# Attention and a two-layer network on one core: broadcast rows joined in one DRAM tile and fetched piece by piece behind the output's stores, and the float32 weight words stored after the split

## The chip, the core and the metric

The kernel runs on one core of a Trainium2 chip. A core has five engines that run their own instruction streams and meet only at semaphores: TensorE (PE in the profile, with its weight loads as PEld), VectorE (DVE), ScalarE (ACT), GpSimd (POOL) and SyncE (SP), which here does nothing but issue DMAs. All but three small loads at the start are issued by SP, in program order: a DMA that has to wait for a semaphore holds up every DMA behind it in SP's queue. The metric is the device time of one execution in microseconds (us), and less is better.

## The reference, cut to what matters

```python
# q, k, v: (4, 8, 768, 64); proj: (64, 6); moe_w_in: (512, 2048); moe_w_out: (2048, 512)
q_bits = (np.einsum('bhsd,dk->bhsk', q, proj) > 0); k_bits = ...   # 6 bits give a bucket
mask = q_bucket[:, :, :, None] == k_bucket[:, :, None, :]
scores = np.where(mask, scale * np.matmul(q, k.transpose(0, 1, 3, 2)), -1000000000.0)
attn = softmax(scores)                     # with 1e-09 added to the sum
attn_out = np.matmul(attn, v)
x = attn_out.transpose(0, 2, 1, 3).reshape(4 * 768, 512)
h = x @ w_in
g = np.where(h >= 1, h, np.where(h <= -1, 0.0, (h + 1) ** 2 / 4))
out = g @ w_out
```

The weights come as float64 and every product is formed from operands that are split into a rounded part and a remainder (hi and lo), so that one float32 product is three TensorE products.

## The kernel before, in words

**Attention.** 32 heads run one after another, each in 12 units (`NU`), about 14 us a head. At fixed units a list of tasks is worked off: moving the next pairs' operands (`move`, L154), putting the row maxima in place (`max_put`, L278: the row that the scores' second matmul needs, `t<-te`, and a copy to DRAM, `ed<-te`), and converting weights (`WeightSplit.steps`, L55). A conversion loads 64-bit words (`s0`), turns them into float32 in `wsq` with four DVE operations and one ACT operation (`s1` to `s4`), rounds (`s5`, ACT) and takes the remainder (`s6`, POOL). With `keep`, the float32 words are stored to DRAM too (`put`, L95, `wq<-wsq`), right behind `s4`. The twelve conversions with `keep` (L997) start at unit 0 of an odd head, and their `put` lies at unit 16 from there, which is unit 4 of the next, even head. Unit 3 of that head has two `move` of 384 KB each, and unit 5 has `max_put`.

**What attention leaves.** The unnormalised output goes to DRAM tiles `x_d[b]`, the maxima's rows to `e_d[b]`, and the inverse of the sums to `r_d[b]` (`sums_inv`), one row of 768 for each of 8 heads. The network's input is (x + e * sv) * r (`make`, L547, and `x_norm`, L698). For that the rows of e and r are read back spread over 64 partitions each: `load_er` (L533) and `x_er` (L689), one DMA of 96 KB for each of e and r, of two heads and of four pieces of 384 tokens, so 16 DMAs a call of `x_er`.

**Network, first stage** (L837, about 484 to 619 us). Chunks of 384 tokens; the first two chunks take 32 steps of 12 matmuls `h` (`gemm1`) and 9 matmuls `y` (L669) that lag three steps. ACT forms t and z from h (`act_in`, L625), DVE squares and adds (`act_out`, L632), ACT rounds (`g_hi`), DVE takes the remainder (`g_lo`). Before each step n the list `prep[n]` is worked off, after it `post[n]`.

**Network, second stage** (L876, 168 products k = 0 to 167, about 619 us to the end). The other six chunks, two a batch of 56 products; a group of seven products (s = 0 to 6, Strassen-like, with sums of operands) makes two blocks of h. Each product is six matmuls, then five or six `y` matmuls of earlier blocks. Two PSUM banks `hb` alternate, so a product needs what DVE or ACT reads two products before. The weights of each product (256 KB) come through a ring of nine buffers (`w_load`, L775).

**Order around the change.** `x_plan` (L719) puts the making of a batch's operands into `prep` and `post`: `x_raw` (four loads of x into `pc[0..3]`) and `x_er` at one place, `x_norm` for the four pieces, then sums, roundings and remainders at the places `made`. In the second stage x_raw and x_er stand at product 3 and 30 of the 56 (L828), `x_norm` from 4 products later, at every second product. When a chunk's `y` is complete, `flush` (L647) copies it from PSUM to SBUF on ACT and stores it (`out_dram<-ot`, 256 KB). For the first two chunks it has two buffers for three copies; later it has four buffers for six copies. The last two chunks' copies of a stage fall at products 4 and 5 (end of the first stage), and at products 2 to 5 of the next 56 (end of a batch).

SP's order inside a step is: the ring's load, the tasks of `prep`, then the stores of `flush`. Each DMA of `x_er` takes SP about 0.6 us to issue.

Of the kernel before, what the change touches and what calls it, by code (L numbers as in the profile page):

```python
# [22 lines left out]
P = 128  # L23
# [18 lines left out]
class WeightSplit:  # L42
# [10 lines left out]
    def steps(self, src, shape, hi, lo, cp, stage=None, low=None, keep=None):  # L53
# [43 lines left out]
        if stage is None:  # L97
            return [s0, s1, s2, s3, s4] + ([put] if keep is not None else []) + [s5, s6]
# [406 lines left out]
class XMaker:  # L505
# [3 lines left out]
    def __init__(self, nc, x_d, s_d, e_d, r_d):  # L509
        self.nc, self.x_d, self.s_d, self.e_d, self.r_d = nc, x_d, s_d, e_d, r_d  # L510
        self.sv, self.er, self.raw = {}, {}, {}

    def sums_load(self, sm, em, b):
# [3 lines left out]
        nc.sync.dma_start(out=self.em, in_=self.e_d[b].rearrange("h (a f) -> (h a) f", f=NF))  # L517
# [56 lines left out]
def ffn(ctx, tc, wpair, woh, wol, xm, xa, xb, areas, wst, wq, wc, out, prep, post):  # L574
# [13 lines left out]
    pc = [xp.tile([P, CH], F32, name=f"pc{i}") for i in range(6)]  # L588
# [20 lines left out]
    def spread(b, cc, k, t):  # L609

        n = 2 * k + t
        if b > 1:
            return sets[(b - 1) % 2][(14, 15, 16, 17, 18, 19, 25, 26)[n]].bitcast(F32)
        if cc == 1:
            return cut(ta, n).bitcast(F32)
        return cut(tflat, n).bitcast(F32) if n < 5 else cut(sflat, n - 5) if n < 7 else pc[5]
# [64 lines left out]
    def x_raw(b, cc):  # L681
# [435 lines left out]
```

## Time and profile before

| | |
|---|---|
| median of 3 runs | 1033.53 us (1033.2, 1033.53, 1037.53) |
| profiled execution: its time, its span | 1037.66 us, 1035.9 us |
| granted TensorE clock, mean | 0.99 |
| DMA: bytes, share of 16 engines | 166.19 MB, 56.6% |
| loads of the broadcast rows (`x_er`) | 96 DMAs of 96 KB |
| loads of the broadcast rows (`load_er`) | 32 DMAs of 96 KB |
| stores of the float32 words with `keep` | 12 of 16 `wq<-wsq` |
| busy share PE, DVE, ACT, POOL | 95%, 77%, 66%, 33% |

The profile comes from one execution; its span leaves out 1.8 us of that execution's time. A timeline row gives start, duration, engine, source line and output<-input; in square brackets stands the engine's idle time before it and what ended it. A row of waits gives the total, the number and the longest of the waits of one kind. A row of a stage gives the stage, its length, the busy time of each engine with the number of instructions, and then the granted TensorE clock, the DMA engines' share and GB/s.

### The profile page before, as it was taken

To read this page: it belongs to the slowest core of one execution; us is meant where nothing else is said; L and a number is where in the kernel's file an instruction comes from. 1 tells how busy PE (TensorE), PEld (TensorE's weight loads), DVE (VectorE), ACT (ScalarE), POOL (GpSimd) and SP (SyncE) were. 2 spreads that over 40 slices of the span, in tenths; PEclk is the share of its full clock that TensorE was granted. 3 is DMA by queue.
4 is the path that set the end of the run, shared out by engine and by line. 5 is a ranking of instruction groups with operands and counts; after the bars stand their busy time and mean duration, and the time that the engine had idled before them with its cause. 6 is when DMAs were issued, how large, how long until landed. Compare 5 with 4: busy or idle time off the path is not lost.

```text
span 1035.9 us, 15651 instructions
## 1 busy us (share of the span) xinstructions
PE 979.7 (95%) x5036; PEld 895.1 (86%) x5036; DVE 793.9 (77%) x1356; ACT 680.9 (66%) x1489; POOL 343.5 (33%) x412
## 2 busy tenths in 40 slices
PE   5899999999999999999998996999996999999997
PEld 4789989899999999989997885888986888988896
DVE  7678989899999998885878983877764767755553
ACT  5779878898989888887545563454553554554444
POOL 6667767777778777565000000000000000000000
PEclk9999999999999999999999998999998999999999
DMA  2645657676656666635376477667456455454331
GB/s 91 171 111 149 170 158 190 169 184 165 179 160 180 159 171 163 152 105 167 95 223 226 143 235 239 206 209 259 122 143 199 117 171 154 119 176 122 113 92 61
DMA packets 95449, 166.19 MB, mean 160 GB/s; under 512 B 15112, under 2 KB 52616, under 8 KB 95368
## 3 DMA queue, kind: packets, MB, share of 16 engines
q1 hardware_dynamic: 95152, 165.20, 56.6%
q8 instruction: 40, 0.66, 0.3%
q14 instruction: 41, 0.34, 0.1%
q10 hardware_dynamic: 216, 0.00, 0.0%
HBM read 106.13 MB, written 33.87 MB: 135 GB/s over the span
## 4 chain that ended last, share of the span: by engine, by line
PE 66%; DVE 10%; DMA 8%; ACT 7%; SPq 5%; issue 2%; POOL 1%; ACTq 0%; DVEq 0%
PE y L669 19%; PE h L892 14%; PE smax L258 5%; PE s L298 5%; PE o L332 5%; PE o L330 5%; PE o L331 5%; PE s L297 4%; DMA t<-te 4%; PE h L801 4%; SPq L695 3%; DVE nm L262 2%; DMA wraw<-in_w_in_dram 1%; DVE t L634 1%; ACT t L628 1%
## 5 line engine op out<-in xcount | busy, mean ns | idle before, releaser
L306 ACT ACTIVATE ph<-s 128x384 fp32r<-128x384 f32 x380 | 188.0, 495 | 55.3 <-PE s L298 47.8
L262 DVE TENSOR_REDUCE nm<-smax 128x1 f32<-128x768 f32 x186 | 176.4, 948 | 26.9 <-PE smax L258 25.4
L39 POOL TENSOR_TENSOR pl<-pf,ph 128x384 fp32r<-128x384 f32 x128 | 140.3, 1101 | 87.7 <-ACT pf L311 83.5
L634 DVE SCALAR_TENSOR_TENSOR t<-t 128x384 f32<-128x384 f32 x128 | 71.4, 557 | 107.2 <-ACT z L629 107.0
L39 DVE TENSOR_TENSOR pl<-s,ph 128x384 fp32r<-128x384 f32 x256 | 135.8, 545 | 14.7 <-ACT s L311 11.0
L669 PE MATMUL y<-t,ghi 128*128 128x512 f32 x384 | 126.5, 401 | 17.5 <-ACT ghi L639 17.4
L298 PE MATMUL s<-t 128*128 128x384 f32 x384 | 131.8, 343 | 6.2 <-DMA t<-te 6.0
L297 PE MATMUL s<-t 128*128 128x384 f32 x384 | 132.4, 345 | 0.8 <-DVE t L212 0.8
L332 PE MATMUL o<-pl,va 128*128 128x386 f32 x384 | 130.8, 341 | 0.2 <-DVE pl L39 0.2
L330 PE MATMUL o<-ph,va 128*128 128x386 f32 x384 | 130.6, 340 | 0.0
L331 PE MATMUL o<-ph,vb 128*128 128x386 f32 x384 | 130.1, 339 | 0.0
L311 ACT ACTIVATE s<-s 128x384 f32<-128x384 f32 x252 | 125.3, 497 | 0.0
L258 PE MATMUL smax<-t 128*128 128x384 f32 x372 | 101.5, 354 | 5.3 <-DVE nm L262 4.6
L669 PEld LDWEIGHTS y<-t,ghi 128*128 128x128 f32 x384 | 72.3, 191 | 29.3 <-ACT ghi L639 18.8
L639 ACT CAST ghi<-z 128x384 fp32r<-128x384 f32 x129 | 65.2, 506 | 34.0 <-DVE z L635 31.6
L643 DVE TENSOR_TENSOR glo<-z,ghi 128x384 fp32r<-128x384 f32 x128 | 70.4, 550 | 19.3 <-ACT ghi L639 19.3
L892 PE MATMUL h<-wbig,t 128*128 128x384 f32 x399 | 82.6, 340 | 0.5 <-DVE wsq L911 0.5
L258 PEld LDWEIGHTS smax<-t 128*128 128x128 f32 x372 | 64.5, 190 | 20.3 <-DVE nm L262 19.0
L629 ACT ACTIVATE z<-t,m 128x384 f32<-128x384 f32 x128 | 79.0, 617 | 4.2
L628 ACT ACTIVATE t<-wsq,mh 128x384 f32<-128x384 f32 x48 | 29.6, 617 | 79.1 <-DVE wsq L905 46.1
L298 PEld LDWEIGHTS s<-t 128*128 128x128 f32 x384 | 72.6, 189 | 10.3 <-DMA t<-te 10.3
L892 PEld LDWEIGHTS h<-wbig,t 128*128 128x128 f32 x399 | 72.3, 190 | 6.6 <-DVE wsq L911 1.4
(150 smaller groups left out, 2113.2 us busy)
## 6 DMA issues: line engine op xcount, KB each, us to landing
t<-wc SPq DMA_DIRECT2D x92, 256.0 KB
t<-t SPq DMA_DIRECT2D x60, 384.0 KB
wraw<-wc SPq DMA_DIRECT2D x76, 256.0 KB
raw<-in_qk_dram SPq DMA_DIRECT2D x15, 768.0 KB
wraw<-in_w_in_dram SPq DMA_DIRECT2D x16, 512.0 KB
wraw<-in_w_out_dram SPq DMA_DIRECT2D x16, 512.0 KB
xd<-xs SPq DMA_DIRECT2D x32, 192.5 KB
vraw<-in_v_dram SPq DMA_DIRECT2D x16, 384.0 KB
```

Source lines behind the costliest of these rows:

```text
L39: eng.tensor_tensor(out=out, in0=a, in1=b, op=ALU.subtract)
L258: nc.tensor.matmul(out=smax[hd][:, hf, 0:HS], lhsT=t2[:, 0, h, i * P:(i + 1) * P], rhs=t2[:, 1, h, hf * HS:(hf + 1) * HS], start=True, sto ...
L262: nc.vector.tensor_reduce(out=nmp(hd)[:, i:i + 1], in_=smax[hd][:, :, 0:HS], axis=AX.XY, op=ALU.max, negate=True)
L297: nc.tensor.matmul(out=ps[:, 0:HS], lhsT=t1[:, 1, h, ks], rhs=t1[:, 0, h, sl], start=True, stop=False)
L298: nc.tensor.matmul(out=ps[:, 0:HS], lhsT=t2[:, 1, h, ks], rhs=t2[:, 0, h, sl], start=False, stop=True)
L306: nc.scalar.activation(out=ph[:, 0:HS], in_=ps[:, 0:HS], func=AF.Exp, scale=SCALE)
L311: nc.scalar.activation(out=pf, in_=ps[:, 0:HS], func=AF.Exp, scale=SCALE)
L330: nc.tensor.matmul(out=o, lhsT=wa, rhs=ph, start=(jj == 0), stop=False)
L331: nc.tensor.matmul(out=o, lhsT=wb, rhs=ph, start=False, stop=False)
L332: nc.tensor.matmul(out=o, lhsT=wa, rhs=pl, start=False, stop=(jj == NJ - 1))
L669: nc.tensor.matmul(out=ys[c][m], lhsT=g_[:, m * P:(m + 1) * P], rhs=w, start=(first and k == 0), stop=(last and k == 2))
L892: nc.tensor.matmul(out=ps, lhsT=w[:, cs], rhs=x, start=(n == 0 and s not in (2, 3, 6)), stop=(n == 5), skip_group_check=True)
```

## The change

Four things are done.

1. `e_d[b]` and `r_d[b]` become the two halves of one DRAM tile `er_d[b]` of shape [8, 2, 768]. A piece's rows e and r of one head are then one DMA of 192 KB, so a call for a piece issues two DMAs in place of four. The SBUF targets are pairs of neighbouring blocks; the six tiles `pc` become one tile `pcs` with six slices, and `x_raw` issues two loads of 384 KB in place of four of 192 KB.
2. `x_er` works one piece k, and `x_plan` takes a place for each: 11, 12, 13, 14 in place of four at 11; 24, 24, 25, 25 in place of 24; in the second stage t, t+1, t+2, t+3.
3. In the second stage t goes from 3 and 30 to 7 and 31. `x_norm` stands at t+4 to t+7 in place of t+4, t+6, t+8, t+10, and `made` at t+9+2k in place of t+12+2k: places 16 to 28 (before 15 to 27) and 40 to 52 (before 42 to 54).
4. `put` with `keep` moves behind `s5` and `s6`: from unit 16 to unit 21, that is from unit 4 to unit 9 of the even head.

```diff
@@ WeightSplit.steps
-            return [s0, s1, s2, s3, s4] + ([put] if keep is not None else []) + [s5, s6]
+            return [s0, s1, s2, s3, s4, s5, s6] + ([put] if keep is not None else [])
@@ XMaker
-        nc.sync.dma_start(out=self.em, in_=self.e_d[b].rearrange("h (a f) -> (h a) f", f=NF))
+        nc.sync.dma_start(out=self.em, in_=self.er_d[b][:, 0].rearrange("h (a f) -> h a f", f=NF))
...
-        nc.sync.dma_start(out=self.r_d[b].rearrange("h (a f) -> (h a) f", f=NF), in_=sm)
+        nc.sync.dma_start(out=self.er_d[b][:, 1].rearrange("h (a f) -> h a f", f=NF), in_=sm)
...
-    def load_er(self, c, ct, eb, rb):
-        b, sl = c // 2, slice(c % 2 * CH, (c % 2 + 1) * CH)
+    def load_rows(self, b, ct, k, er):
+
         for h in range(2):
-            rs = slice(64 * h, 64 * h + 64)
-            r = 2 * ct + h
-            self.nc.sync.dma_start(out=eb[rs], in_=self.e_d[b][r:r + 1, sl].partition_broadcast(64))
-            self.nc.sync.dma_start(out=rb[rs], in_=self.r_d[b][r:r + 1, sl].partition_broadcast(64))
-        self.er[c, ct] = (eb, rb)
+            src = self.er_d[b][2 * ct + h:2 * ct + h + 1, :, k * CH:(k + 1) * CH]
+            self.nc.sync.dma_start(out=er[64 * h:64 * h + 64], in_=src.rearrange("o t n -> (o t) n").partition_broadcast(64))
+
+    def load_er(self, c, ct, er):
+        self.load_rows(c // 2, ct, c % 2, er)
+        self.er[c, ct] = (er[:, 0], er[:, 1])
@@ ffn
-    pc = [xp.tile([P, CH], F32, name=f"pc{i}") for i in range(6)]
+    pcs = xp.tile([P, 6, CH], F32, name="pcs")
+    pc = [pcs[:, n] for n in range(6)]
...
-        for k in range(4):
-            sl = slice(k // 2 * CH, (k // 2 + 1) * CH)
-            nc.sync.dma_start(out=pc[k], in_=xm.x_d[b][:, 2 * (k % 2) + cc, sl])
-
-    def x_er(b, cc):
-        for k in range(4):
-            ct, sl = 2 * (k % 2) + cc, slice(k // 2 * CH, (k // 2 + 1) * CH)
-            for t, d in enumerate((xm.e_d[b], xm.r_d[b])):
-                for h in range(2):
-                    r = 2 * ct + h
-                    nc.sync.dma_start(out=spread(b, cc, k, t)[64 * h:64 * h + 64],
-                                      in_=d[r:r + 1, sl].partition_broadcast(64))
+        for k in range(2):
+            nc.sync.dma_start(out=pcs[:, 2 * k:2 * k + 2], in_=xm.x_d[b][:, cc::2, k * CH:(k + 1) * CH])
+
+    def x_er(b, cc, k):
+        xm.load_rows(b, 2 * (k % 2) + cc, k // 2, spread(b, cc, k))
@@ x_plan and its calls
         at(raw, x_raw, b, cc)
-        at(er, x_er, b, cc)
         for k, n in enumerate(norm):
             at(n, x_norm, b, cc, k)
+            at(er[k], x_er, b, cc, k)
...
-    x_plan(1, 0, 11, 11, (13, 14, 15, 16), (17, 17, 18, 18, 19, 19, 20))
-    x_plan(1, 1, 22, 24, (26, 26, 27, 27), (28, 28, 29, 29, 30, 30, 31))
+    x_plan(1, 0, 11, (11, 12, 13, 14), (13, 14, 15, 16), (17, 17, 18, 18, 19, 19, 20))
+    x_plan(1, 1, 22, (24, 24, 25, 25), (26, 26, 27, 27), (28, 28, 29, 29, 30, 30, 31))
     for b in (2, 3):
         for cc in range(2):
-            t = N1 + 56 * (b - 2) + (3, 30)[cc]
-            x_plan(b, cc, t, t, [t + 4 + 2 * k for k in range(4)], [t + 12 + 2 * k for k in range(7)])
+            t = N1 + 56 * (b - 2) + (7, 31)[cc]
+            x_plan(b, cc, t, [t + k for k in range(4)], [t + 4 + k for k in range(4)],
+                   [t + 9 + 2 * k for k in range(7)])
@@ lsh_attn_ffn
-    e_d = [xdp.tile([H, S], F32, name=f"ed{b}") for b in range(B)]
+    er_d = [xdp.tile([H, 2, S], F32, name=f"ed{b}") for b in range(B)]
+    e_d = [t[:, 0] for t in er_d]
...
-        conv((2 * i + 3) * NU, wi_steps(i, nc.scalar), (0, 7, 9, 13, 15, 16, 17, 19))
+        conv((2 * i + 3) * NU, wi_steps(i, nc.scalar), (0, 7, 9, 13, 15, 17, 19, 21))
```

`spread` chooses the same SBUF memory for the rows as before in batches 2 and 3 and in the second call of batch 1. In the first call of batch 1 the third and fourth pieces move by one block, so that each pair is contiguous.

More of the change, by code (lines that the diff above doesn't have):

```diff
@@ L505, with __init__ @@
 class XMaker:
[L509 to L510 removed]
+    def __init__(self, nc, x_d, s_d, er_d):
+        self.nc, self.x_d, self.s_d, self.er_d = nc, x_d, s_d, er_d
         self.sv, self.er, self.raw = {}, {}, {}
@@ L952, in lsh_attn_ffn @@
     wc = [xdp.tile([P, NBLK, 2, DM // 2], F32, name=f"wc{i}") for i in range(NFT // 2)]
-    r_d = [xdp.tile([H, S], F32, name=f"rd{b}") for b in range(B)]
-    xm = XMaker(nc, x_d, s_d, e_d, r_d)
+    xm = XMaker(nc, x_d, s_d, er_d)
     def flat(t):
@@ L1028, in load_er @@
     def load_er(c, ct):
-        xm.load_er(c, ct, *(t[:, ct].bitcast(F32) for t in (xa, xb)[c]))
+        er = flat((T2[i0], T2[i1])[c]).rearrange("p (t c n) -> p t c n", t=2, c=NCT)
+        xm.load_er(c, ct, er[:, :, ct].bitcast(F32))
     at(g0 + 2, load_raw)
```

21 lines of the change are left out of this document (12 added, 9 removed).

## The prediction

> **What bounds the kernel now.** The page first: who is busy, and at what clock.
>
> ```profile
> span 1035.9 us, 15651 instructions
> PE 979.7 (95%) x5036; PEld 895.1 (86%) x5036; DVE 793.9 (77%) x1356; ACT 680.9 (66%) x1489; POOL 343.5 (33%) x412
> PEclk9999999999999999999999998999998999999999
> ```
>
> PE is busy 95% of the span and works in order, so wherever it stands still time is lost. The clock dips in two slices, the 25th (from 622 us) and the 31st (from 777 us). The lists of waits say why: first PE's own in the network (540 us to the end), then two of ACT's over the whole span, then one of attention.
>
> ```profile
> PE y L669 <- ACT ghi L639: 18.2, 3, 9.6
> PE h L801 <- ACT t L628: 2.9, 1, 2.9
> PE h L892 <- DVE wsq L911: 2.6, 4, 1.1
> ...
> ACT ot L658 <- DMA out_dram<-ot: 24.7, 3, 10.4
> ACT wsq L69 <- DMA wraw<-in_w_out_dram: 10.5, 1, 10.5
> ...
> PE s L298 <- DMA t<-te: 6.0, 11, 2.2
> ```
>
> PE waits for ACT, and ACT was waiting for a store of the output or for a weight load. The timelines of PE, ACT and SP give the places. The rows stand by place: PE's wait, ACT's, then what SP was issuing.
>
> ```profile
> 645.46 1.22 PE L669 MATMUL y<-t,ghi 128*128 128x512 f32 x2 [9.57 <-ACT ghi L639]
> 630.53 0.57 ACT L658 COPY ot<-y 128x512 f32<-128x512 f32 x1
> 633.48 0.57 ACT L658 COPY ot<-y 128x512 f32<-128x512 f32 x1
> 644.41 0.58 ACT L658 COPY ot<-y 128x512 f32<-128x512 f32 x1 [10.36 <-DMA out_dram<-ot]
> 627.61 1.12 SPq L695 DMA_DIRECT2D t<-ed  x2
> ...
> 640.16 0.38 SPq L659 DMA_DIRECT2D out_dram<-ot  x1
> ...
> 786.41 1.22 PE L669 MATMUL y<-t,ghi 128*128 128x512 f32 x2 [7.88 <-ACT ghi L639]
> 785.37 0.58 ACT L658 COPY ot<-y 128x512 f32<-128x512 f32 x1 [9.06 <-DMA out_dram<-ot]
> 771.94 1.09 SPq L695 DMA_DIRECT2D wbig<-ed  x2
> ...
> 782.35 0.53 SPq L659 DMA_DIRECT2D out_dram<-ot  x1
> ...
> 548.90 2.35 PE L801 MATMUL h<-t,wbig 128*128 128x384 f32 x12 [2.92 <-ACT t L628]
> 547.70 0.68 ACT L69 ACTIVATE wsq<-wraw 128x512 f32<-128x512 f32 x1 [10.54 <-DMA wraw<-in_w_out_dram]
> 532.52 1.11 SPq L695 DMA_DIRECT2D tmp<-ed  x2
> ...
> 542.71 0.51 SPq L62 DMA_DIRECT2D wraw<-in_w_out_dram  x1
> ```
>
> Read the first place: the copy of 630.53 can be stored from 631.1 on, but SP is issuing `x_er` from 627.61 and comes to the store only at 640.16. The third copy needs that buffer, so ACT is blocked for 10.36 us, and PE runs out of rounded operands. The second place is the same, with the second store (782.35), which the sixth copy needs. At the third a weight load stands behind `x_er`, from 532.52 to 542.71.
>
> The kernel has its own control: at the beginning of the last batch six copies and stores fall as at the second place, but there is no `x_er` ahead of them. Here is that stage, and those of the three restarts:
>
> ```profile
> 895.00:917.00 22.00, 22.00 (x111) 19.72 (x110) 13.80 (x27) 14.54 (x28) 0.00 (x0) 1.00 0.59 184
> ...
> 645.00:650.50 5.50, 5.04 (x14) 4.43 (x15) 4.39 (x9) 2.82 (x6) 0.00 (x0) 0.53 1.04 344
> 786.00:791.50 5.50, 5.09 (x17) 4.59 (x18) 4.43 (x9) 2.78 (x6) 0.00 (x0) 0.63 1.01 368
> 548.00:552.00 4.00, 3.10 (x16) 2.71 (x17) 3.90 (x8) 3.89 (x8) 0.00 (x0) 1.00 1.08 365
> ```
>
> In the control PE is busy for all of the 22.00 us. Its 111 matmuls, 11 a product, also give a product's length: 2.2 us. After the two long stops PE restarts at a granted clock of 0.53 and 0.63, after the stop of 2.92 us at 1.00.
>
> **The change, part by part.** The sum is made against the profiled execution (1037.66 us).
>
> *Stores ahead of the rows.* The last store is issued at product 5, and `x_raw` and the first piece now stand at 7. The second place becomes the control: its 7.88 us go, and so does the slow restart, 5.50 us x (1 - 0.63) = 2.0. At the first place there are two buffers for three copies, so the third still waits for the first store. That is ready at 631.1, SP then has only the ring's loads and two loads of weight words, and ACT is blocked from 634.05, the end of the second copy. How long a store takes to land:
>
> ```profile
> 640.16 4.17 DMA out_dram<-ot
> ...
> 603.97 0.59 ACT L658 COPY ot<-y 128x512 f32<-128x512 f32 x1 [5.26 <-DMA out_dram<-ot]
> ```
>
> The chain gives 4.17 us; three copies back to back in the first stage waited 5.26. The buffer is then free at 635.3 to 636.4, and ACT waits 1.3 to 2.4 us. PE's stop was 0.8 us shorter than ACT's (9.57 against 10.36), so it stops for 0.5 to 1.6; I take 1.0. Saved here: 9.57 - 1.0, and the restart, 5.50 x (1 - 0.53) = 2.6. The two places: 11.2 + 9.9 = 21.1 us.
>
> The Trainium skill (TensorE: Matmul & The Clock Gate, Part 1) says that the clock is halved after about 3.4 us of idling and comes back after as much busy time. The trace agrees: 2.92 us cost no clock, 7.88 us did. By the page's figures a restart loses an estimated 1.7 us, 3.4 for two, where the rows give 4.6.
>
> *Pieces in the first stage.* Only the first piece's two DMAs now precede the load of 542.71. It goes out some 8 us sooner: the 10.2 us from 532.52, less 1.1 to 2.2 for the first piece. ACT stopped 10.54 us and PE 2.92, so 7.6 us of ACT's stop are covered, and less than that is left. The 2.92 us go. Next in line: the fourth piece, at step 14, now stands behind a weight load that waits for its buffer, and its `x_norm` comes two steps of 4.2 us later. DVE may wait there for a microsecond; the `y` matmuls' lag of three steps hides it. I cost it at nothing; uncovered, 1 us.
>
> *Joined DMAs.* The bytes are the same with half the issues. Two single issues take SP 1.1 us now (771.94); a joined pair, with twice the rows, takes 1.1 to 2.2. At one pair a product even that is no more than the product, and the ring's loads behind it are up to nine products ahead: nothing. `load_er` halves in attention, where no row shows PE waiting for it: nothing.
>
> *`put` from unit 4 to unit 9 of the even head.* In attention PE waits for `t<-te`; first SP's rows of the worst case, then three of PE's waits.
>
> ```profile
> 127.09 1.18 SPq L95 DMA_DIRECT2D wq<-wsq  x1
> 128.37 1.95 SPq L282 DMA_DIRECT2D t<-te  x1
> ...
> 134.66 0.62 PE L298 MATMUL s<-t 128*128 128x384 f32 x1 [2.20 <-DMA t<-te]
> ...
> 62.06 0.44 PE L298 MATMUL s<-t 128*128 128x384 f32 x1 [0.41 <-DMA t<-te]
> ...
> 206.67 0.44 PE L298 MATMUL s<-t 128*128 128x384 f32 x1 [0.78 <-DMA t<-te]
> ```
>
> `put` takes 1.18 us of SP and lays 256 KB just ahead of the row. Of the eleven waits, those at 62.06 and 206.67 close heads without a moved `put`; the other nine hold 6.0 - 0.41 - 0.78 = 4.8 us. The row goes out 1.3 us sooner (128.37 - 127.09) and finds 256 KB less ahead of it. The bounds are 0, if the two `move` set its landing, and 4.8. I take 4.0: but for the 2.20 the waits average 0.3 us, well under 1.3. At its new place `put` waits for nothing, as s4 is long done; behind it are loads for later heads. It holds its `wsq` buffer five units longer, and that is used again only 24 units after.
>
> *`x_norm` at consecutive products.* This costs. It stands at s = 4, 5, 6, 0 of the groups (products 11 to 14), before at s = 0, 2, 4, 6. DVE works in order, and cv (L908, s = 5), ACT, `act_out`, cu (L911, s = 6) are a chain that PE needs at the second product of the next group. With an `x_norm` at s = 6:
>
> ```profile
> 801.39 0.56 DVE L634 SCALAR_TENSOR_TENSOR t<-t 128x384 f32<-128x384 f32 x1 [1.33 <-ACT z L629]
> ...
> 802.47 0.61 DVE L700 SCALAR_TENSOR_TENSOR pc<-wbig,xsvb,pc 128x384 f32<-128x384 f32 x1
> ...
> 803.59 0.55 DVE L911 TENSOR_TENSOR wsq<-h,wsq 128x384 f32<-128x384 f32 x1
> ...
> 664.38 1.31 PE L892 MATMUL h<-wbig,t 128*128 128x384 f32 x6 [0.26 <-DVE wsq L911]
> ```
>
> One `x_norm` takes 803.59 - 802.47 = 1.12 us. With it L911 ends where PE wants it: at 804.14 PE does not wait, and in the batch before, where weight work stands beside it, it waits 0.26. The second one, at s = 5, lies wholly in this chain: 1.1 us in each of two batches at most, and I take 2.0 in all. The batches' second calls have two `x_norm` ahead of L899 as before: nothing. Bounds 0 and 5 (DVE's slack used up, and 1 us more in each of three groups).
>
> The sum: -11.2 - 9.9 - 2.9 - 4.0 + 2.0 = -26.0 us, or 1011.7 in the profiled execution. The median of the runs is 4.1 us lower and would give 1007.5. Whether the removed waits are those 4.1 us the profile cannot say; I forecast the middle, **1009.5 us**.
>
> **Rivals.** *Rows late.* As a mechanism: over four products (8.8 us) x, rows and the ring bring 0.8 + 1.5 + 1.0 = 3.3 MB, which take 9 us at the 368 GB/s of the stage above; each piece has four products to arrive and just holds. If they come 3 us late in each of two batches, DVE and then PE wait: 1015.5. The Trainium skill (DMA: Bandwidth & Descriptors, Rules for kernel authors) speaks for this one: it advises to issue a DMA early and to wait late, and here the rows are issued four products later.
>
> *No gain from `put`*, because the moves set the landing: 1013.5. *The first place keeps 4 us of its stop*, because w_put's 1 MB delays the store: 1012.5. *The change does not do what it says*, stores still being behind the rows: about 1030; the copies of 630.53 and 633.48, two products before the new place, speak against it.
>
> *The other side: `pcs` is tracked as one tile.* Each DVE write into one slice then waits for ACT's last cast out of another. What such a merged tile does, `wbig` shows:
>
> ```profile
> 807.13 0.51 ACT L714 CAST wbig<-pc 128x384 fp32r<-128x384 f32 x1
> ...
> 807.14 0.69 PE L892 MATMUL h<-wbig,wraw 128*128 128x384 f32 x3
> ```
>
> Six plans of seven casts, each 0.51 us with a copy of 0.57 ahead of it, are up to 42 x 1.08 = 45 us, or 1055. It decides from 31 us (26 gained and 5 over), 0.74 us of PE a cast. Against it stands that pair: ACT writes one slice of `wbig` while PE reads another.
>
> **Chances.** The forecast with its terms 0.62; rows late 0.12; no gain from `put` 0.10; first place 0.07; without effect 0.04; one tile 0.05. The range of 80% goes from 1003 (six microseconds from `t<-te` and no cost on DVE: 30 us off the median) to 1020 (nothing from `put`, 5 us on DVE, 1.5 of late rows: 17.5 off the profiled execution). About 0.5%, 5 us, is what a measurement here can tell from no change. Faster by more than that 0.91, within 0.04, slower 0.05.
>
> **What will show it.** PE's waits for ACT's ghi fall from 18.2 to under 3 us; the two dips are gone from the clock's row; in SP's timeline the stores stand ahead of the rows; ACT's wait for the weight load is gone; PE's waits for `t<-te` are under 2 us; those for L911 rise from 2.6 to about 5. Wrong would be DVE's L700 waiting microseconds for the rows, or DVE's writes into `pc` waiting for ACT.

## The result, and the profile after

The changed kernel takes 1010.90 us (median of 4 runs, 1010.01 to 1011.32), the kernel before 1033.37 us (median of 4, 1032.68 to 1037.53). The ratio is 0.9773, with a 95% interval from 0.9747 to 0.9800. The profiled execution after took 1011.32 us, 26.3 less than the one before (1037.66). In what follows, "after" is the changed kernel, and its line numbers are its own: `h` is L799 in the first stage and L891 in the second, `y` L674, `x_norm` L698 and L700, the loads of the rows L537, the copy and the store of the output L663 and L664.

The page of after, the same rows that were shown of before:

```profile
span 1009.5 us, 15524 instructions
PE 973.4 (96%) x5036; PEld 889.6 (88%) x5036; DVE 797.7 (79%) x1356; ACT 680.9 (67%) x1489; POOL 341.7 (34%) x412
PEclk9999999999999999999999999999999999999999
```

The two dips of the clock are gone. Next the list of waits of after, first PE's own in the network (540 us to the end), then rows of the list for the whole span (total us, times, longest):

```profile
PE h L891 <- DVE wsq L910: 4.6, 4, 1.6
PE h L891 <- DVE wa L907: 2.2, 2, 1.4
PE h L891 <- DVE wsq L904: 1.6, 1, 1.6
PE y L674 <- ACT ghi L644: 1.1, 2, 0.7
```

```profile
DVE pcs L698 <- DMA t<-ed: 3.5, 1, 3.5
DVE pcs L698 <- DMA tmp<-ed: 3.4, 1, 3.4
ACT wsq L69 <- DMA wraw<-in_w_out_dram: 3.2, 1, 3.2
DVE pcs L698 <- DMA wbig<-ed: 2.3, 1, 2.3
ACT ot L663 <- DMA out_dram<-ot: 2.2, 1, 2.2
...
PEld s L298 <- DMA t<-te: 0.2, 1, 0.2
```

PE's 18.2 us behind ACT's `ghi` have become 1.1, ACT's 24.7 us behind the output's store 2.2, and attention's wait for `t<-te` has gone. What is new stands beside them: DVE waits for the broadcast rows (`t<-ed`, `wbig<-ed`, and in the first stage `tmp<-ed`), and PE for three DVE instructions in a row, L904, L907 and L910. SP's timeline at the first place says what happened to the order:

```profile
617.76 0.34 SPq L664 DMA_DIRECT2D out_dram<-ot  x1
...
620.71 1.59 SPq L664 DMA_DIRECT2D out_dram<-ot  x2
622.39 1.36 SPq L775 DMA_DIRECT2D t<-wc  x2
...
624.38 1.27 SPq L691 DMA_DIRECT2D pcs<-xd  x2
625.70 1.26 SPq L537 DMA_DIRECT2D t<-ed  x2
```

The stores stand ahead of x and rows, as the change intends. The price is in the chain of work that ended last, at the first pieces of the two batches; a DMA's row there runs from its issue to its landing:

```profile
626.35 7.44 DMA t<-ed
...
633.93 0.63 DVE pcs L698
...
761.08 6.70 DMA wbig<-ed
...
767.81 0.63 DVE pcs L698
```

Each of these two rows is one DMA of 192 KB of a pair; it takes 7.44 and 6.70 us to land. The view by stages shows why the first can be slow: around it all 16 DMA engines are full (last but one column), and move little for that (GB/s, the last one).

```profile
618.00:623.00 5.00, 5.00 (x26) 4.45 (x25) 2.96 (x6) 3.67 (x7) 0.00 (x0) 1.00 0.88 289
623.00:628.00 5.00, 5.00 (x27) 4.54 (x27) 4.32 (x9) 3.13 (x8) 0.00 (x0) 1.00 1.05 332
628.00:634.00 6.00, 6.00 (x30) 5.06 (x28) 2.42 (x6) 1.07 (x3) 0.00 (x0) 1.00 1.06 240
634.00:640.00 6.00, 3.08 (x14) 2.36 (x14) 4.71 (x9) 1.52 (x3) 0.00 (x0) 1.00 1.08 242
```

From 634 to 640 us PE is busy for 3.08 of 6.00 us. DVE's timeline there, and then PE's with its waits, show the stop from instruction to instruction:

```profile
633.93 0.62 DVE L698 SCALAR_TENSOR_TENSOR pcs<-t,xsva,pcs 128x384 f32<-128x384 f32 x1 [3.55 <-DMA t<-ed]
634.58 0.56 DVE L700 TENSOR_TENSOR pcs<-pcs,t 128x384 f32<-128x384 f32 x1
635.06 0.55 DVE L904 TENSOR_TENSOR wsq<-h,wa 128x384 f32<-128x384 f32 x1
...
639.13 0.55 DVE L907 TENSOR_TENSOR wa<-wa,h 128x384 f32<-128x384 f32 x1
...
643.20 0.55 DVE L910 TENSOR_TENSOR wsq<-h,wsq 128x384 f32<-128x384 f32 x1
```

```profile
635.66 1.31 PE L891 MATMUL h<-wbig,t 128*128 128x384 f32 x6 [1.56 <-DVE wsq L904]
639.73 1.31 PE L891 MATMUL h<-wbig,t 128*128 128x384 f32 x6 [1.35 <-DVE wa L907]
643.81 1.34 PE L891 MATMUL h<-wbig,t 128*128 128x384 f32 x6 [1.60 <-DVE wsq L910]
```

The first `x_norm` is 3.55 us late, L904 comes right behind it, and PE's product s = 6 starts when L904 ends. From there L904, L907 and L910 are 4.07 us apart. The same three in the last batch, where no `x_norm` stands between them, are 2.96 and 2.95 us apart:

```profile
895.82 0.56 DVE L904 TENSOR_TENSOR wsq<-h,wa 128x384 f32<-128x384 f32 x1 [1.54 <-PE h L891]
...
898.78 0.55 DVE L907 TENSOR_TENSOR wa<-wa,h 128x384 f32<-128x384 f32 x1
...
901.73 0.55 DVE L910 TENSOR_TENSOR wsq<-h,wsq 128x384 f32<-128x384 f32 x1
```

The difference, 1.11 us, is one `x_norm` (1.12 in the prediction's rows). So two things cost time here, rows that land late and `x_norm` in the chain.

For the experiments one number is used throughout: the **loss** of a stretch, how much later its products start than at full pace. Full pace is 2.205 us from the start of one product to the next (1.99 for products 3 to 5 of the whole stage, which carry four `y` matmuls, and 2.44 for s = 6, with six). Over the last 55 products of after, which hold no preparation, the loss by this is 0.31 us. In after product 12 starts at 631.71 and product 13 at 635.66, which makes 3.95 - 2.205 = 1.74 us of loss, counted at product 12. By stretches, in us:

| products | what stands there | before | after |
|---|---|---|---|
| 4 to 10 | first place | 12.07 | 0.11 |
| 11 to 17 | `x_norm`, batch 2 | 0.64 | 5.51 |
| 18 to 24 | sums, roundings, weights | 0.61 | 1.41 |
| 63 to 66 | second place | 9.86 | 0.02 |
| 67 to 76 | `x_norm`, batch 3 | 0.11 | 3.13 |

### The profile page after: what moved, and what is told of

It is laid out like the page before. It is cut to its first block, busy times and chain, and to the rows that moved or that the text cites. A ratio compares the mean times of both kernels' runs of the same rounds, so it can differ in the third digit from the quotient of the medians.

```text
span 1009.5 us, 15524 instructions
## 1 busy us (share of the span) xinstructions
PE 973.4 (96%) x5036; PEld 889.6 (88%) x5036; DVE 797.7 (79%) x1356; ACT 680.9 (67%) x1489; POOL 341.7 (34%) x412
## 4 chain that ended last, share of the span: by engine, by line
PE 76%; DVE 11%; ACT 5%; DMA 5%; issue 2%; SPq 1%; POOL 0%; ACTq 0%; DVEq 0%
PE y L674 18%; PE h L891 13%; PE smax L258 7%; PE o L332 6%; PE o L330 6%; PE s L298 6%; PE o L331 6%; PE s L297 6%; PE h L799 4%; DMA t<-ed 2%; PE o L178 2%; DVE nm L262 2%; DVE t L639 1%; ACT t L633 1%; ACT z L634 1%
## 5 line engine op out<-in xcount | busy, mean ns | idle before, releaser
L674 PE MATMUL y<-t,ghi 128*128 128x512 f32 x384 | 124.7, 395 | 0.4 <-ACT ghi L644 0.4
L891 PE MATMUL h<-wbig,t 128*128 128x384 f32 x399 | 82.2, 338 | 5.3 <-DVE wsq L910 2.4
L891 PEld LDWEIGHTS h<-wbig,t 128*128 128x128 f32 x399 | 70.9, 188 | 12.9 <-DVE wsq L910 3.4
L674 PEld LDWEIGHTS y<-t,ghi 128*128 128x128 f32 x384 | 71.3, 188 | 11.6 <-ACT ghi L644 0.9
L674 PE MATMUL y<-woh,glo 128*128 128x512 f32 x192 | 75.9, 395 | 1.1 <-DVE glo L648 1.0
L674 PE MATMUL y<-woh,ghi 128*128 128x512 f32 x192 | 75.6, 394 | 0.7 <-ACT ghi L644 0.7
```

Of the source, the lines that this page charges most:

```text
L674: nc.tensor.matmul(out=ys[c][m], lhsT=g_[:, m * P:(m + 1) * P], rhs=w, start=(first and k == 0), stop=(last and k == 2))
L891: nc.tensor.matmul(out=ps, lhsT=w[:, cs], rhs=x, start=(n == 0 and s not in (2, 3, 6)), stop=(n == 5), skip_group_check=True)
```

## The experiments

Two theories were to be told apart. **Rows**: the rows land late because they queue behind the output's stores and the weight words, and each microsecond of it reaches PE. **Chain**: `x_norm` at four consecutive products costs this by itself, on time or not. Beside it stood the question how much of the gain is `put`, and what joining the DMAs is worth.

### `put` alone

The kernel before, with `put` moved and nothing else.

```diff
-            return [s0, s1, s2, s3, s4] + ([put] if keep is not None else []) + [s5, s6]
+            return [s0, s1, s2, s3, s4, s5, s6] + ([put] if keep is not None else [])
...
```

> The kernel before with the store of the float32 words moved to unit 21 and nothing else. If attention's gain is the store's (theory), the network starts 8.9 us sooner as in the changed kernel (its fourth step's matmuls at 482 us, before at 491), PE does not wait for t<-te, and the three stops in the network stay: about 1024.5 us, a ratio near 0.991. Rival: the joined row loads in attention's end or something else gives part of it; then the start moves by less than 8 us.

Measured: 1028.10 us (1027.87 to 1028.60), before beside it 1033.97, ratio 0.9948 (0.9933 to 0.9964). `put` gives 5.9 us, by the interval 3.7 to 6.9, and not the 9 that were expected. In the profiles the fourth step of the network does start 10.0 us sooner (481.13, before 491.09), but the profiled execution of before was one of its longer ones. This run's profile has no wait of PE for `t<-te` left, and 0.6 us of the weight loads'. The three stops in the network stay (ACT waits 23.7 us for the store and 11.1 for the weight load).

### The places alone

The kernel before with x and rows behind the stores, `x_norm` at consecutive products and `made` as in the change; single DMAs, all sixteen at one place.

```diff
-            t = N1 + 56 * (b - 2) + (3, 30)[cc]
-            x_plan(b, cc, t, t, [t + 4 + 2 * k for k in range(4)], [t + 12 + 2 * k for k in range(7)])
+            t = N1 + 56 * (b - 2) + (7, 31)[cc]
+            x_plan(b, cc, t, t, [t + 4 + k for k in range(4)], [t + 9 + 2 * k for k in range(7)])
```

> The kernel before with the second stage's places alone (7 and 31, x_norm and made as in the changed kernel), the rows still in single DMAs of 96 KB, all sixteen at one place. If the order behind the stores is what removes the two long stops, both are gone (22 us less) and only the costs behind it remain, attention and the 2.9 us of the first stage as before: 1015 to 1020 us. Rival: the joined pieces are needed too; then 10 us of issues at product 7 hold up the ring's loads or the later pieces and PE stands still for 5 us and more: over 1022 us.

Measured: 1021.96 us (1020.48 to 1023.51), ratio 0.9888 (0.9869 to 0.9908), 12.0 us less than before, and 2 us above what was expected. The two long stops are gone. The first-stage stop stays (ACT waits 11.5 us for its weight load, PE 3.88). The losses where `x_norm` stands are 3.20 and 1.69 us, with DVE's waits for rows as follows (its timeline):

```profile
642.73 0.62 DVE L700 SCALAR_TENSOR_TENSOR pc<-t,xsva,pc 128x384 f32<-128x384 f32 x1 [1.19 <-DMA t<-rd]
...
778.12 0.62 DVE L700 SCALAR_TENSOR_TENSOR pc<-wbig,xsvb,pc 128x384 f32<-128x384 f32 x1 [0.88 <-DMA wbig<-ed]
```

Both numbers come back in the table below. Beside them products 18 to 24 lose 4.28 us, and DVE waits 2.77 there for the store of the weights' sums (`wc<-sumw`); after loses 1.40 there. Attention is that of before, and this execution gives a second look at it; the fourth step of the network, before and here:

```profile
491.09 2.36 PE L801 MATMUL h<-t,wbig 128*128 128x384 f32 x12 [1.57 <-ACT t L628]
```

```profile
487.91 2.36 PE L801 MATMUL h<-t,wbig 128*128 128x384 f32 x12 [1.66 <-ACT t L628]
```

With the same code this step came 3.18 us sooner than in the profiled execution of before.

### `x_norm` with a product between, in the first calls

After, with `x_norm` at 11, 13, 15, 17 in both batches' first calls.

```diff
-            x_plan(b, cc, t, [t + k for k in range(4)], [t + 4 + k for k in range(4)],
+            x_plan(b, cc, t, [t + k for k in range(4)], [t + 4 + (2 - cc) * k for k in range(4)],
```

> The changed kernel with x_norm of the first calls at products 11, 13, 15, 17 in place of 11 to 14; rows, stores and everything else as there. The changed kernel loses 5.5 us at products 11 to 17 of the first batch and 3.1 in the second. Theory of the chain (x_norm at s = 4, 5, 6 one behind the other): s = 5 is free again and about 3 us come back, 0.6 and 0.1 us are left if the rows are on time. Theory of the late rows: DVE still waits 3.5 and 2.3 us for the first piece, so 2 us or more stay lost at products 12 and 13 of the first batch. 1006 to 1008 us by the first, 1009 by the second.

Measured: 1010.32 us (1009.89 to 1012.74), ratio 0.9780 (0.9761 to 0.9800): no change that can be told. The first `x_norm` still waits, 3.37 and 1.81 us; the losses are 4.24 (products 11 to 17), 2.52 (18 to 24) and 1.51 (67 to 76). In the first batch what the chain gives back (1.3 us) comes out again in the next group (1.1); the late rows stay. The loss less the wait is 0.87 and -0.30 here, where it is 1.96 and 0.80 in after: taking `x_norm` off s = 5 takes 1.1 us from each batch's stretch, one `x_norm`.

### Rows one product sooner

After, with x and rows of the first calls at 6 to 9 in place of 7 to 10, `x_norm` where it was.

```diff
-            x_plan(b, cc, t, [t + k for k in range(4)], [t + 4 + k for k in range(4)],
+            x_plan(b, cc, t - 1 + cc, [t - 1 + cc + k for k in range(4)], [t + 4 + k for k in range(4)],
```

> The changed kernel with x_raw and the rows of the first calls one product sooner (6 to 9 in place of 7 to 10), still behind the last store; x_norm stays at 11 to 14. Theory of the late rows: DVE's waits for the first piece (3.5 and 2.3 us) fall by up to 2.2 us, and 1 to 3 us come back over the two batches. Theory of the chain: the loss at products 11 to 17 stays within half a microsecond of 5.5 and 3.1. If the DMA engines are full in either case, the waits fall by less than the 2.2 us.

Measured: 1008.27 us (1007.81 to 1008.69), ratio 0.9757 (0.9739 to 0.9776). The median is 2.6 us below that of after, but the intervals overlap, and of the 3.5 us between the two profiles 2.5 had been gained before product 0, where the kernels are the same. In the second batch DVE waits 1.20 us in place of 2.33, and the loss is 2.00 in place of 3.13: the one falls by as much as the other. In the first batch nothing moves (3.61 and 5.56). SP's timeline and the chain of this run say why:

```profile
618.23 1.58 SPq L664 DMA_DIRECT2D out_dram<-ot  x2
...
622.71 1.26 SPq L537 DMA_DIRECT2D t<-ed  x2
```

```profile
623.36 8.01 DMA t<-ed
```

SP goes from the stores over one ring load and x straight to the rows, so they can't start much sooner: 20.3 us after product 0 (623.36 - 603.05), in after 20.8 (626.35 - 605.53). That half microsecond is lost again in landing, 8.01 against 7.44 us.

### `x_norm` off the chain

After, with `x_norm` of the first calls three products later, at 14 to 17 (s = 0 to 3).

```diff
-            x_plan(b, cc, t, [t + k for k in range(4)], [t + 4 + k for k in range(4)],
+            x_plan(b, cc, t, [t + k for k in range(4)], [t + (7, 4)[cc] + k for k in range(4)],
```

> The changed kernel with x_norm of the first calls three products later, at 14 to 17 (s = 0, 1, 2, 3), rows unmoved at 7 to 10. There the chain cv, act_out, cu has no x_norm in it, and the rows have seven products to arrive. If the loss at products 11 to 23 (6.9 us in the first batch, 3.1 in the second) is that chain and the wait for the first rows, both theories have most of it come back: 2 us or less left in the first batch, 0.3 in the second, about 1004 us. If a DVE backlog is only moved to s = 1 (L899) and s = 3 (L902), 3 us or more stay in the first batch.

Measured: 1011.11 us (1009.57 to 1012.40), ratio 0.9774 (0.9747 to 0.9801), as after. DVE waits for no row, and the losses at `x_norm` are 0.12 and 0.37 us. But products 18 to 24 now lose 9.16: 6.3 in one stop of PE and 2.8 right behind it, where the granted clock is halved (0.51 from 651.6 to 658.5 us). PE stands behind a DVE that waits for a store: the sums of weights that some products need are written to DRAM (`wc<-sumw`), and the next sums can't go into that memory sooner (DVE's timeline, then PE's):

```profile
646.81 0.69 DVE L39 TENSOR_TENSOR sumw<-tmp 128x512 f32<-128x512 f32 x1 [4.71 <-DMA wc<-sumw]
```

```profile
652.59 2.29 PE L891 MATMUL h<-wbig,wraw 128*128 128x384 f32 x6 [6.15 <-DVE wa L902]
```

So the first batch isn't mended by moving `x_norm` alone, and the 1004 us of both theories don't come: the DMA engines are as full (1.08 from 628 to 640 us), and the next transfer is late instead. In the second batch products 77 to 79 lose 0.9 us that they do not lose in after.

### Single DMAs

After, with the joined DMA of e and r of a head split into two again.

```diff
-            src = self.er_d[b][2 * ct + h:2 * ct + h + 1, :, k * CH:(k + 1) * CH]
-            self.nc.sync.dma_start(out=er[64 * h:64 * h + 64], in_=src.rearrange("o t n -> (o t) n").partition_broadcast(64))
+            for t in range(2):
+                src = self.er_d[b][2 * ct + h:2 * ct + h + 1, t, k * CH:(k + 1) * CH]
+                self.nc.sync.dma_start(out=er[64 * h:64 * h + 64, t], in_=src.partition_broadcast(64))
```

> The changed kernel with the rows of e and r fetched by separate DMAs of 96 KB again, piece by piece at the same places. Run e2_place_alone, with single loads, had the DMA engines at a share of 0.55 to 0.63 while rows came, and DVE waited 1.2 us for the first rows; joined they are at 1.06 to 1.08 and DVE waits 3.5. If joining makes the first rows late, DVE's waits fall to 1 to 2 us and the losses at products 11 to 17 from 5.5 and 3.1 to about 3.3 and 1.7: some 3 us off, 1008. If it is the bytes asked for in these products, the waits stay above 3 and 2 us and the time within 1 us of 1010.9. In the first stage the piece takes twice the issues; the stop stays gone by either.

Measured: 1011.71 us (1011.07 to 1012.59), ratio 0.9779 (0.9759 to 0.9800). Against after's 0.9773 this is no difference. The waits for rows are 2.28 and 2.34 us, the losses 4.26 and 3.14, and products 18 to 24 lose 3.75, with a wait of DVE of 2.28 us for the store of the weights' sums. More issues do not make the rows later: in the first batch they even come 1.3 us sooner, and the time is lost again behind that store. Neither expectation holds as written.

### `put` in two parts

After, with an eighth of `put`'s bytes at unit 16, the old place, and the rest at unit 21.

```diff
-            return [s0, s1, s2, s3, s4, s5, s6] + ([put] if keep is not None else [])
+            return [s0, s1, s2, s3, s4] + ([put_a, s5, s6, put_b] if keep is not None else [s5, s6])
...
```

> The changed kernel with the store of the float32 words cut in two: an eighth of the columns at the old place, unit 16, the rest at unit 21. The old place then costs SP its issue again but lays only 32 KB ahead of the maxima's row. If the 256 KB ahead of the row made PE wait, the time is that of the changed kernel, 1010.9 within 1 us, and PE waits under 1 us for t<-te. If it is SP's 1.2 us of issue, most of the 5.9 us that e1_put_alone gained is lost: 1014 to 1017, with t<-te waits of 3 us and more.

Measured: 1013.22 us (1011.66 to 1013.75), ratio 0.9791 (0.9769 to 0.9813). An issue with an eighth of the bytes brings back 1.4 us of PE's waits for `t<-te` (4 times) and 3.3 of the weight loads' (6), of 6.0 and 10.3 before. By these waits the larger part was the bytes; what is left is the issue with its 32 KB, which this run does not take apart. In time the difference from after lies within the intervals.

### The first stage's rows in one go

After, with the four pieces of the first-stage call all at step 11, joined.

```diff
-    x_plan(1, 0, 11, (11, 12, 13, 14), (13, 14, 15, 16), (17, 17, 18, 18, 19, 19, 20))
+    x_plan(1, 0, 11, (11, 11, 11, 11), (13, 14, 15, 16), (17, 17, 18, 18, 19, 19, 20))
```

> The changed kernel with the four pieces of the first call of the first stage all at step 11 again, joined. Half the issues are ahead of the weight load then, some 5 us in place of 10. ACT's wait for the load was 10.5 us before and is 3.2 in the changed kernel; PE's stop was 2.9 us, with 7.6 us of ACT's wait covered. By that cover ACT waits 7 to 8.5 us here and PE stops for under 1 us: joining alone does nearly all of it, 1011 to 1012. Rival: the place of the pieces is what counts, and PE stops for 2 us and more: 1013 and over.

Measured: 1012.97 us (1011.46 to 1014.47), ratio 0.9791 (0.9766 to 0.9816). ACT's wait for the weight load is 8.3 us (10.5 before, 3.2 after), but PE's stop there, 2.92 us before, is 0.65 us (its timeline at 536.27). Half the issues would nearly have done; what taking them piece by piece adds is too small for the times to tell.

### Rows spread further, two versions

The first version moves x and rows of the first batch five products on and spreads them over products 12 to 18, with `x_norm` at 16, 18, 20, 22; in the second batch `x_norm` goes to s = 6, 0, 1, 2 of the groups (products 13 to 16 of the batch). The second version makes only the second of these two edits.

```diff
-            t = N1 + 56 * (b - 2) + (7, 31)[cc]
-            x_plan(b, cc, t, [t + k for k in range(4)], [t + 4 + k for k in range(4)],
-                   [t + 9 + 2 * k for k in range(7)])
+            t = N1 + 56 * (b - 2) + ((12, 33), (7, 31))[b - 2][cc]
+            w, m, o = ((2, 2, 7), (1, 1, 9))[b - 2] if cc == 0 else (1, 1, 9)
+            x_plan(b, cc, t, [t + w * k for k in range(4)], [t + 4 + 2 * (b == 3 and cc == 0) + m * k for k in range(4)],
+                   [t + o + 2 * k for k in range(7)])
```

> The changed kernel with other places in the second stage. First batch, first call: x and rows from product 12 on, a piece every second product (12, 14, 16, 18), x_norm at 16, 18, 20, 22, made at 19 to 31; its second call at 33, x_norm at 37 to 40, made at 42 to 54. Second batch, first call: rows at 7 to 10 as in the changed kernel, x_norm at 13 to 16. Theory of full DMA engines: from product 4 to 16 of the first batch stores, weight words, ring and rows ask for some 9 MB in 27 us, and e5_norm_off_chain only moved the wait from the rows to the store of the weight words' sums. With the rows behind that, the 6.9 us lost at products 11 to 24 fall to 3 or less; in the second batch 3.1 fall to 0.5 (x_norm at one place of the chain, rows in time). About 1005 us. If DVE's own work is the cause and not the transfers, the first batch still loses 5 us and more, at other products: 1008 to 1010.

> The changed kernel with x_norm of the second batch's first call at products 13 to 16 in place of 11 to 14 and nothing else. It has no weight work beside it. Both theories: the rows have two products more (DVE's wait of 2.3 us goes) and s = 5 has no x_norm; the loss of 3.1 us at products 11 to 20 of that batch falls to 0.5, the first batch keeps its 6.9: 1008 us. If 2 us or more stay in the second batch, the chain reading is wrong.

Measured: 1006.76 us (1006.04 to 1008.57), ratio 0.9731 (0.9702 to 0.9760), for the first; 1009.43 (1008.90 to 1010.20), ratio 0.9754 (0.9722 to 0.9787), for the second. The first has the lowest median of the kernels that do the whole work. Its interval overlaps that of after; in the profiles its second stage is 3.5 us shorter (from the first product to the end 1005.0 - 604.55 = 400.45, after 1009.5 - 605.53 = 403.97). In both, the second batch loses 1.2 to 1.3 us in place of 3.13, and no row is waited for there; 0.5 was expected. In the first batch of the first version no row is late either, and products 11 to 17 lose 0.10; but products 18 to 24 lose 5.31 us, where 3 or less was expected for both stretches. PE's waits there are for DVE's results of the group again, the longest three in its timeline:

```profile
647.63 1.33 PE L892 MATMUL h<-wbig,wraw 128*128 128x384 f32 x6 [0.98 <-DVE wa L903]
653.37 1.31 PE L892 MATMUL h<-wbig,wraw 128*128 128x384 f32 x6 [0.77 <-DVE wa L908]
657.92 1.31 PE L892 MATMUL h<-wbig,t 128*128 128x384 f32 x6 [1.69 <-DVE wsq L911]
```

### Half the bytes of the rows

Two more kernels ask how much of the rest is bytes: after, and the spread version above, with the rows of batch 2's first call sent to 32 of 64 partitions. Instructions and their order stay.

```diff
...
-            self.nc.sync.dma_start(out=er[64 * h:64 * h + 64], in_=src.rearrange("o t n -> (o t) n").partition_broadcast(64))
+            self.nc.sync.dma_start(out=er[64 * h:64 * h + np], in_=src.rearrange("o t n -> (o t) n").partition_broadcast(np))
...
```

> The changed kernel, but the rows of the first call of batch 2 (places 7 to 10) go to 32 of their 64 partitions only: the same eight DMAs, half the bytes, 0.75 MB in place of 1.5; the other partitions keep what was there. The instructions and their order are unchanged. Theory A, the DMA engines are full there and the rows come by their bytes: 0.75 MB less at the 240 GB/s of that stage are 3.1 us, about DVE's wait of 3.55 us; that wait falls under 1 us, the engines' share in 628 to 640 us falls under 1, the loss over products 11 to 17 falls from 5.5 to under 2.5 us, and the time by about 3 us to 1008. Theory B, the x_norm in the chain of DVE cost this by themselves: the loss stays at 4 to 5.5 us and the time at 1011. Theory C, the rows wait for SP's issues or a fixed latency: the wait stays above 2.5 us, since the issues are as many.

> The version with the rows spread over products 12 to 18, with the same half of the bytes of that one call (32 of 64 partitions). There the loss left in the first batch stands at products 18 to 24 (5.3 us), and DVE waits 4.1 us for the load of the weight sums. Theory A: with 0.75 MB less that wait falls under 2 us, the loss of products 18 to 24 falls under 3.5, and the time from 1006.8 to about 1004.5. Theory B: x_norm stands at s = 2, 4, 6 and 1 of the groups there, and the loss is theirs: it stays at 4.5 to 5.3, the time at 1006 to 1007.

Measured: 1010.10 us (1007.08 to 1011.08), ratio 0.9752 (0.9732 to 0.9772), and 1006.28 us (1005.43 to 1006.98), ratio 0.9723 (0.9706 to 0.9739). None of the three theories of the first holds as written. DVE's wait falls from 3.55 to 2.02 us, not under 1, and the loss from 5.51 to 3.99:

```profile
630.06 0.62 DVE L698 SCALAR_TENSOR_TENSOR pcs<-t,xsva,pcs 128x384 f32<-128x384 f32 x1 [2.02 <-DMA t<-wc]
```

The `t<-wc` named in it is a ring load that this instruction does not read; the profile names what ended last. The share of the DMA engines from 628 to 640 us is 0.92 to 0.93 (1.06 to 1.08 after). Bytes are thus a part of the lateness, 1.5 us for half of this call's; 2.0 us remain that stand behind other transfers or SP's queue.

In the second kernel, as its theory B said, the time is that of the spread version and most of the loss stays. DVE's wait for the store of the weights' sums falls from 3.33 to 2.64 us (its timeline with full rows, then with half):

```profile
643.44 0.69 DVE L39 TENSOR_TENSOR sumw<-tmp 128x512 f32<-128x512 f32 x1 [3.33 <-DMA wc<-sumw]
```

```profile
642.14 0.69 DVE L39 TENSOR_TENSOR sumw<-tmp 128x512 f32<-128x512 f32 x1 [2.64 <-DMA wc<-sumw]
```

The loss of products 18 to 24 falls from 5.31 to 4.62 by the same 0.69 us, all of it at product 18: products 20 and 21 lose 0.97 and 2.34 with half the rows, 0.96 and 2.34 with full ones. Here too the loss is the wait plus a constant, 1.98 us. DVE's sums, remainders and `x_norm` stand in the chain there, and no run takes them apart.

### What all of them say together

Put side by side, the kernels that keep the four consecutive `x_norm` from s = 4 on agree on one relation. The wait is that of the first `x_norm` in DVE's timeline, the loss that of products 11 to 17 and 67 to 76:

| kernel | first batch: wait, loss, loss - wait | second batch: wait, loss, loss - wait |
|---|---|---|
| places alone | 1.19, 3.20, 2.01 | 0.88, 1.69, 0.81 |
| half the bytes | 2.02, 3.99, 1.97 | 1.86, 2.67, 0.81 |
| single DMAs | 2.28, 4.26, 1.98 | 2.34, 3.14, 0.80 |
| after | 3.55, 5.51, 1.96 | 2.33, 3.13, 0.80 |
| rows one product sooner | 3.61, 5.56, 1.95 | 1.20, 2.00, 0.80 |
| first stage in one go | 3.87, 5.82, 1.95 | 1.47, 2.27, 0.80 |
| spread, second batch only | 3.75, 5.71, 1.96 | (moved) |
| `put` in two parts | 4.39, 6.36, 1.97 | 2.07, 2.87, 0.80 |

Over waits from 0.88 to 4.39 us the loss is the wait plus a constant, 1.95 to 2.01 us in the first batch and 0.80 to 0.81 in the second. So both theories were right, each with its own share, and they add: a microsecond of late rows costs PE a microsecond, and what stands beside it is a constant however late the rows are. That this constant is the chain is shown in part: without `x_norm` at s = 5 it is 1.1 us less in each batch. No run has four consecutive `x_norm` from s = 4 on and no wait at all. In after the rows make 3.55 + 2.33 = 5.9 us and the constants 2.0 + 0.8 = 2.8, of which the kernel before, with `x_norm` spread out and on time, had 0.64 + 0.11 = 0.75.

## Why the prediction was right, point by point

The time fell where the forecast put it, 1010.9 against 1009.5 us. Its terms were not all right: one was missing and one too small, and the two nearly cancelled. That the sum came out is luck to that extent. Profiled execution against profiled execution, in us:

| step | predicted | measured | from |
|---|---|---|---|
| first place | -11.2 | -12.0 | loss of products 4 to 10 |
| second place | -9.9 | -9.8 | loss of products 63 to 66 |
| stop in the first stage | -2.9 | -4.2 | from the fourth step to product 0, 127.80 to 123.59 |
| `put` | -4.0 | -9.2 | start of the fourth step, 491.09 to 481.94 |
| `x_norm` in the chain | +2.0 | +2.0 | the constants above, less 0.75 of before |
| rows late | 0 (rival: 6) | +5.9 | DVE's two waits |
| rest of the second stage | 0 | +0.9 | what the stage's -13.0 leaves |
| sum | -26.0 | -26.4 | the spans: 1035.9 to 1009.5 |

**Stores ahead of the rows** went as worked out: both stops and both slow restarts are gone, and "places alone" gets them without the rest. The microsecond that the first place was to keep is not there (0.11). ACT does wait 2.2 us, inside the 1.3 to 2.4 given; but PE's operands lasted.

**The first stage**: the stop is gone, and the 1.3 us beyond the forecast were not traced to rows. The same stretch takes 122.81 to 123.95 us in the eight other runs with after's first stage, and 128.36 and 128.78 in the two with that of before, so some of it is the scatter of one execution. The DVE wait that `y`'s lag should hide came at the first piece, not at the fourth: 3.35 us at 530.15, and none at the fourth (544.49). PE has no wait there, so the cover held for more than the microsecond that was costed.

**Joined DMAs** at nothing: right in time, by the run with single ones.

**`put`** was mis-sized, and the step that failed is its upper bound, 4.8 us. By the run of `put` alone the median falls by 5.9 us, and the interval, 3.7 to 6.9, does not decide against the bound; the profiles do. In the eleven kernels with the whole `put` moved the fourth step starts at 480.24 to 481.94; in "places alone", with attention as before and no wait of PE for `t<-te` longer than 0.8 us (4.1 in all), at 487.91. That is 6.0 to 7.7 us, 6.8 for `put` alone. The bound counted PE's own idle time only; the weight loads had waited longer at the same places (10.3 us, 13 times, and 8.3 in "places alone"), and they go too. That they make up the difference is not shown by itself. The 9.2 of the table holds more: in the profiled execution of before one wait, the 2.20 us, cost 3.9 (last section), and "places alone" came out of attention 3.18 us sooner. That may answer most of the 4.1 us between before's profiled execution and the median, which the prediction had left open: it would be one event of attention, which went with the removed waits. There is no second profile of before, so this rests on that one comparison.

**`x_norm` in the chain**: 2.0 us, as taken. The prediction gave one `x_norm` of 1.1 us to each batch, the one at s = 5; the run with a product between shows that one, 1.1 us in each. Over before, which spreads them otherwise, the constants make 1.3 in the first batch and 0.7 in the second, so the fit of the sum is closer than its argument.

**Rows late** was priced as a rival (3 us in each of two batches) with a chance of 0.12, and it came true: 3.55 and 2.33 us. The step of the forecast that failed is the sentence that "each piece has four products to arrive and just holds". It divided 3.3 MB by 368 GB/s, the rate of a stage with full-width transfers; with broadcast rows among them the full engines move 240 GB/s (628 to 640 us), by which 3.3 MB take 13.8 us, not 9. It also let the rows start at product 7, which begins at 620.59, where SP issued the second DMA of the first piece at 626.3, behind the stores, two ring loads and x. How the lateness divides between the two the runs show only in part: half the bytes take 1.5 of the 3.55 us away. Late issue was what the Trainium skill (DMA: Bandwidth & Descriptors, Rules for kernel authors) spoke against; the trace agrees here, with 5.9 us.

What the prediction named as proof did show: `ghi` under 3 us, the dips gone, stores ahead of rows, L910 at 4.6 (about 5 was said), no wait of PE for `t<-te`. One did not: ACT's wait for the weight load was to be gone, and 3.2 of its 10.5 us are left, which cost PE nothing. There was also what it named as the sign of being wrong: DVE waiting microseconds for the rows. `pcs` is not tracked as one tile: no wait of DVE for ACT's cast came up in the lists.

## What to carry to other kernels

When a transfer is moved behind others to let them go first, price its own arrival again at the new place: count SP's issues ahead of it and use the rate of a stage with the same kind of transfers, since lateness can reach the busiest engine one to one. To size a wait that goes away, look at the weight loads' waits as well, and don't take the matmuls' alone for an upper bound. And check a forecast that hits by its terms: here a missing +5.9 and a gain too small by 5.2 hid each other.

## What the runs showed of the hardware that was not expected

A short stop can cost clock. Before's wait of 2.20 us is followed by matmuls of 0.52 us where they take 0.34, and the stage's granted clock is 0.60, although the stop of 2.92 us before 548.90 was followed by a clock of 1.00. PE's timeline and the view by stages of before:

```profile
132.12 0.34 PE L297 MATMUL s<-t 128*128 128x384 f32 x1
...
135.07 0.52 PE L330 MATMUL o<-ph,va 128*128 128x386 f32 x1
...
138.24 0.33 PE L297 MATMUL s<-t 128*128 128x384 f32 x1
```

```profile
134.00:138.00 4.00, 3.34 (x11) 3.35 (x12) 1.08 (x2) 1.31 (x4) 2.10 (x4) 0.60 0.96 341
```

From 134.66 to 138.24 PE starts 11 matmuls, 3.58 us where 11 steps of 0.175 us (the pace from 138.24 on) make 1.9; with the wait the event cost 2.20 + 1.65 = 3.9 us. `put` in two parts shows it once more, after a stop of 2.40 us (PE's timeline and a stage):

```profile
637.91 2.29 PE L897 MATMUL h<-wbig,t 128*128 128x384 f32 x6 [2.40 <-DVE wsq L910]
```

```profile
637.00:641.00 4.00, 3.09 (x9) 2.90 (x10) 3.07 (x7) 1.23 (x2) 0.00 (x0) 0.58 1.06 246
```

In the first stage of `put` alone a stop of 3.46 us was followed by a clock of 1.00 (539 to 544 us), in that of "places alone" one of 3.88 by 0.62 (546 to 550.5). The Trainium skill (TensorE: Matmul & The Clock Gate, Part 1) puts the halving after about 3.4 us of idling. The prediction found that the trace agrees, but it had read two stops only; idle times of 2.20 and 2.40 us were enough twice, and the measurement decides. Shorter gaps ahead of the stop are not the reason: PE was busy for 8.94 of the 9 us before the stop of 2.20 (123.46 to 132.46), and for all of 626 to 635.5 before that of 2.40. What decides instead no run here settles.

Stages with broadcast rows show full DMA engines that do not move much: 240 GB/s at a share of 1.06, where a stage of before in which SP issues none of them (645 to 650.5 us) moved 344 at 1.04. Issued one by one all at one place, as in "places alone", they leave the engines at a share of 0.54 to 0.65 (176 to 189 GB/s, 640 to 652 us), and SP takes about 0.6 us for each; single and joined DMAs at the same places, piece by piece, differ in no time that could be measured (1011.71 and 1010.90 us).
